# A delta-rule attention block with a hard-swish layer behind it: b of the later units turned by VectorE from quarter transfers, v fetched a block sooner, outputs in one transfer, scan ends copied by ScalarE

## The chip, the cores and the metric

One core of a Trainium2 chip runs the kernel. The metric is the time of one execution on the device, in microseconds. Before the change it is 775.2 us, the median of three runs (773.38 to 775.27).

The engines are named as in the profile: PE is TensorE (PEld its weight loads), DVE VectorE, ACT ScalarE, POOL GpSimd, SP the engine that issues nearly all transfers.

## The reference

```python
# attention: r, k, v, w, a, b are (4 batches, 8 heads, 768 steps, 40); state is (4, 8, 40, 40), from zero
for t in range(S):
    y[:, :, t] = np.einsum('bhd,bhde->bhe', rt, state)
    Sa = np.einsum('bhde,bhe->bhd', state, at)
    state_decay = state * wt[:, :, None, :] - np.einsum('bhd,bhe->bhde', Sa, bt)
    state = state_decay + np.einsum('bhd,bhe->bhde', vt, kt)
# then, on x = y as (3072 tokens, 320):
h = x @ w_in                                   # 320 -> 2048
out = (h * np.clip(h + 3.0, 0.0, 6.0) / 6.0) @ w_out   # 2048 -> 320
```

## The kernel before

**Units.** The 768 steps are cut into blocks of 64 (BL). A unit is one such block of time for a pair of batches: 128 partitions are 2 batches x 64 steps, and the free axis holds 8 heads x 40 features, padded to 64 a head (SLOT). There are NK = 24 units; unit i has time block 2 (i // 4) + (i % 4) // 2 and batch pair i % 2 (`names`). Four units (NU) make a group.

**What is done to a unit.** `prepare(i, F)` needs no state. W turns w (L506) and takes running products along time with a scan on VectorE (L603). gam scans the other way (L614), in place in the edge tile `wm`, then puts together the decays `gam` (G) and their inverses `rgam`: half of each is copied from `wm` (L626 or L628), half from `prods` by GpSimd (L632, L633). A and B turn a and b so that features lie on partitions and time on the free axis, and multiply by G and rg (`at` L650, `bt` L658). F is the product of at and bt (f_by_64, L685); K turns k (L736); factor turns rgam and makes K and B times decay in KBt (L725, GpSimd); E and EV follow. The triangle in F is inverted for a whole group at once by `invert`, some sixty short VectorE steps (L804, L810) that are dealt out between other work ("aside").

`step(i)` carries the state: RT and VT (turns of r and v), R, C, S, U, UT, rS, H, ysn (state and output), then move and move2: eight transfers on SP (L1111 and L1116) that put the unit's output `yg` into `xt` for the feed-forward part. `open` lets the feed-forward stream use it. C ends with a copy of v by GpSimd (L993).

The feed-forward stream takes each unit's xt in two jobs: `expand` (h = xt times win, L1171; the 64 rows left over, "short", L1171 with 64 rows or L1184), hard swish on ScalarE and VectorE (L1193, L1194), and `contract` (L1219), then ob (L1237) and two output transfers on SP (L1243).

**Order.** The order of all engines is fixed when the program is written out: each engine runs its instructions in that order. From unit 8 on (after some 190 us) the work runs in blocks `a_block(m)`, four blocks a unit. In each block, `together` puts the TensorE products of all stages that are due in the order PRODUCTS, then what follows them on the other engines in the order RESULTS; between the blocks, pieces of the feed-forward stream and steps of the inversion are dealt out (`feed`). A unit u begins at block `begins[u]`, 4 blocks apart from unit 12 on, with stages W and gam in the first block, A and B in the second, F and K in the third, E and factor in the fourth, EV in the fifth. Units from 7 on (FAR) have their xt moved in the block of ysn and opened in the next; units 4 to 6 are moved in the block after ysn, which is the block of A and B of a later unit.

"Short" has two forms. `narrow[0](...)` puts it in a block ahead of the stages of HALVES (VT, B, factor): if the block has one of these, as eight pairs of 64x128 matmuls, otherwise as 64x64 quarters (`fours`, L1184).

**Two ways of turning.** Up to unit 7, and for w, k, v later too, TensorE turns a tile through PSUM (`turn_pairs`, `turn_halves`, L516: eight transposes of 64x64 a unit). From unit 8 on, a and r are loaded by quarters (second part of `fetch`, L478): transfers put runs of 80 or 48 features of each head pair to partitions 0 to 31, 32 to 63 and so on, in such places that one VectorE transpose of 32x32 blocks gives the turned tile (`turn_blocks`, L528, L531). b is also read in its plain form, by KBt.

**Transfers.** SP issues them in the order of the program, and each waits for its tile to be free; a waiting one holds all behind it. `fetch("V", i)` of units 9 and later stands at the end of `k_stage`; the slot of `values` that it fills was unit i - 5's, last read by L993.

Of the kernel before, what the change touches and what calls it, by code (L numbers as in the profile page):

```python
# [8 lines left out]
F32 = mybir.dt.float32  # L9
# [22 lines left out]
def kernel(  # L32
# [151 lines left out]
        nc.vector.memset(low[:, i:i + 1], x)  # L184


    AHEAD, FAR = NU + 1, 2 * NU - 1
    PADS = {"W": 1.0, "V4": 1.0}

    def padded(t, name):  # L190
# [18 lines left out]
    nc.vector.memset(start[:], 0.0)  # L209
    nc.vector.memset(start[:].rearrange("p (n i) -> p n i", i=HB + 1)[:, :, 0:1], 1.0)  # L210
    EDGE = 2 * (SCAN + 1)
    area = const.tile([P, EDGE + 3 * H * BL], F32, name="area")
    wms = [area[:, i * (SCAN + 1):(i + 1) * (SCAN + 1)] for i in range(2)]
    for t in wms:
        nc.vector.memset(t, 0.0)
# [235 lines left out]
    def fetch(name, i, engine=None):  # L451

        if i is None or i >= NK:
            return
        x, crossed = {"W": (w, 0), "A": (a, 0), "B": (b, 0), "K": (k, 0), "R": (r, 1),
                      "V": (v, 1)}[name]
        if name == "V":
            t = values[i % AHEAD]
        else:
            t = placed.get((name, i))  # L460
            if (name, i) == ("R", 1):
                t = others["K"]
            if (name, i) == ("W", NU + 1):
                t = values[NU]
            t = t if t is not None else (others if i < 2 * NU and i % 2 and name != "R" else inputs)[name]
        g, p = names[i]
        engines = engine or nc.sync
        if name == "R" and i >= NU or name == "A" and i >= 2 * NU:
            y = x[2 * p:2 * p + 2, :, g * BL:(g + 1) * BL, :]
            n = 2 if name == "R" else 1  # L470
            y = y.rearrange("q (k s j) t e -> s j (q k) (t e)", s=2, j=n).rearrange(
                "s j k (l e) -> s j l k e", e=2 * D)
            for s in range(2):
                for c in range(0, D, L):
                    z = s * SLOT + c
                    to = rooms[name][z:z + L].rearrange("l (j k e) -> l j k e", j=n, e=2 * D)
                    for j in range(n):
                        nc.sync.dma_start(out=to[:, j, :, 0:2 * D - c], in_=y[s, j, :, :, c:])  # L478
            data[i][name + "N"] = t
            return  # L480
        for q in range(2):
            engine = engines[q] if isinstance(engines, tuple) else engines
            y = x[2 * p + q, :, g * BL:(g + 1) * BL, :]
            rows = slice(q * BL, (q + 1) * BL)
            if crossed:
                for s in range(2):
                    engine.dma_start(out=t[rows, 4 * s:4 * s + 4, 0:D],
                                     in_=y[s::2].rearrange("h t e -> t h e"))
            else:
                engine.dma_start(out=t[rows, :, 0:D], in_=y.rearrange("h t e -> t h e"))  # L490
        data[i][name + "N"] = t
# [32 lines left out]
    def turn_blocks(to, name):  # L524

        x = rooms[name].rearrange("p (j k y e) -> p j k y e", j=2, y=2, e=D)[:, :, :, :, 0:L]
        if name == "A":
            nc.vector.transpose(out=to[:].rearrange("p r (q t y) -> p q r y t", q=2, y=2), in_=x)  # L528
            return
        for j in range(2):  # L530
            nc.vector.transpose(out=to[:, 2 * j:2 * j + 2].rearrange("p r (q t y) -> p q r y t", q=2, y=2),  # L531
                                in_=x[:, j].rearrange("p (q r) y t -> p q r y t", q=2))
# [28 lines left out]

    def begun_beside():

        begin = -(-(SCAN + 1) // 16) * 16
        for n, name in enumerate("KB"):
            x = area[:, begin + n * H * JOIN:begin + (n + 1) * H * JOIN]
            nc.gpsimd.memset(x, 0.0)
            beside[name] = x.rearrange("p (h t) -> p h t", h=H)
        beside["E"] = grp.tile([P, H, BL], F32, name="E", tag="U", bufs=1)
        nc.gpsimd.memset(beside["E"][:], 0.0)  # L570
        for name in "rgam", "RT":
            beside[name] = tmp.tile([P, NPR, P], F32, name=name, tag="rgam", bufs=2)

# [7 lines left out]

    def prepare(i, F):
        n, o = i % NU, data[i]
        halves = i >= 2 * NU
        def w_stage():
            wt = turn_pairs(o["WN"])
            yield PE
# [20 lines left out]
        def gam_stage():  # L608

            prods, wm = o["prods"], o["wm"]  # L610
            first = start[:].rearrange("p (n i) -> p n i", i=HB + 1)[:, :, 0]
            nc.vector.reciprocal(first, prods[:].rearrange("p r m i -> p (r m) i")[:, ::-1, HB])
            back = _ap(wm, SCAN, [[-1, SCAN]])
            nc.vector.tensor_tensor_scan(out=back, data0=back, data1=start[:], initial=0.0,  # L614
                                         op0=ALU.mult, op1=ALU.add)
            nc.vector.memset(first, 1.0)
            gam = o["G"] = grp.tile([P, NPR, P], F32, name="gam", tag="gam", bufs=NU + 2)
            rgam = o["rg"] = beside["rgam"] if halves else placed.get(("rgam", i)) or \
                tmp.tile([P, NPR, P], F32, name="rgam", bufs=2)
            gv = gam[:].rearrange("p r (q i) -> p (r q) i", q=2)  # L620
            rv = rgam[:].rearrange("p r (q i) -> p (r q) i", q=2)
            row = 2 * (HB + 1)

            def copy(to, x):
                if i < NU:
                    nc.scalar.activation(out=to, in_=x, func=AF.Copy)  # L626
                else:
                    nc.vector.tensor_scalar(to, x, 1.0, None, ALU.mult)  # L628

            copy(gv[:, :, 0:HB], _ap(o["wm"], HB + 1, [[row, NB], [-1, HB]]))  # L630
            copy(rv[:, :, HB:BL], _ap(o["wm"], HB + 3, [[row, NB], [1, HB]]))
            nc.gpsimd.tensor_copy(gv[:, :, HB:BL], o["prods"][:, :, 1, 0:HB])  # L632
            nc.gpsimd.tensor_copy(rv[:, :, 0:HB], o["prods"][:, :, 0, 0:HB][:, :, ::-1])  # L633
            dec = grp.tile([P, 2, 2, NPR], F32, name="dec", tag="dec", bufs=NU + 2)
            nc.gpsimd.tensor_copy(dec[:].rearrange("p m q r -> p r q m"),
                                  o["prods"][:].rearrange("p (r q) m i -> p r q m i", q=2)[:, :, :, :, HB])
            o["dec"] = dec
            if NU + 1 < i <= 2 * NU:
                fetch("V", i)
            yield from ()  # L640

        def a_stage():
# [4 lines left out]
            if halves:  # L647
                x = at
                turn_blocks(at, "A")
            nc.vector.tensor_tensor(out=at[:], in0=x[:], in1=o["G"][:], op=ALU.mult)  # L650
            fetch("A", following(i))

        def b_stage():
            x = turn_in(o["BN"], halves)
            yield PE
            bt = o["bt"] = turned("bt")
            for y, z, g in zip(parts_of(bt, halves), x, parts_of(o["rg"], halves)):
                nc.vector.tensor_tensor(out=y, in0=z, in1=g, op=ALU.mult)  # L658

# [72 lines left out]
        def k_stage():  # L732
# [1 line left out]
            yield PE  # L734
            kt = o["kt"] = turned("kt")
            nc.vector.tensor_tensor(out=kt[:], in0=x[:], in1=o["rg"][:], op=ALU.mult)  # L736
            if i > 2 * NU:
                fetch("V", i)

        def e_stage():  # L740
            x = scores(o["kt"], o["at"])
# [3 lines left out]
        def ev_stage():  # L745
# [10 lines left out]
            for x in range(2):  # L756
# [1 line left out]
                                     func=AF.Copy)  # L758
            o["EV"] = EV

        return {"W": w_stage, "gam": gam_stage, "A": a_stage, "B": b_stage, "F": f_by_32 if i < 2 * NU else f_by_64,
                "factor": factor_stage, "K": k_stage, "E": e_stage, "EV": ev_stage}

    def in_turn(stages, order):
# [446 lines left out]
    def contract(i, r, gts):  # L1211
# [19 lines left out]
        else:  # L1231
# [5 lines left out]
                nc.scalar.activation(out=ob[:], in_=op[:], func=AF.Copy, scale=1.0 / 6.0)  # L1237
            del ready[i]
            g, p = names[i]
            for q in range(2):  # L1240
                row = (2 * p + q) * T + g * BL
                queue = nc.scalar if q and i == NK - 1 else nc.sync
                queue.dma_start(out=out[row:row + BL, :], in_=ob[half(q)])  # L1243
        yield True


# [201 lines left out]
    for _ in range(18):  # L1448
# [7 lines left out]
    EARLY_STAGES = [["fade"], ["RT", "VT"]]  # L1456
    OWN_STAGES = EARLY_STAGES + [[], ["R", "C", "S"], ["U", "UT", "rS"], ["H"]]
    NEAR_END, FAR_END = [["ysn"], ["move", "move2"]], [["ysn", "move", "move2"], ["open"]]
    AHEAD_STAGES = [["W", "gam"], ["A", "B"], ["F", "K"], ["E", "factor"], ["EV"]]
    CLOSE_STAGES = [["W", "gam"], ["A", "B"], ["F", "K", "factor"], ["E"], ["EV"]]  # L1460


    PRODUCTS = ["W", "S", "K", "VT", "B", "factor",
                "ysn", "EV", "R", "C", "U", "UT", "rS", "H", "E", "F"]
    RESULTS = ["ysn", "W", "VT", "EV", "R", "S", "C", "A", "B", "move", "move2", "open",
               "U", "UT", "rS", "F", "K", "fade", "H", "E", "factor", "RT", "gam"]
    TURNS = PRODUCTS[:3]
    WIDTH = {"R": NPR * D, "U": 512, "UT": 0, "ysn": NPR * JOIN, "EV": NPR * D}
# [40 lines left out]
    def a_block(m):  # L1509

        if coming and begins[coming[0]] == m:
            u = coming.popleft()
            close = coming and begins[coming[0]] < m + BLOCKS
            ahead[u, m] = prepared(u), CLOSE_STAGES if close else AHEAD_STAGES
        i, early = (m + len(EARLY_STAGES)) // BLOCKS + NU, m + len(EARLY_STAGES)
        if m >= 0 and early % BLOCKS == 0 and i < NK:
            own[i, m] = step(i), OWN_STAGES + (NEAR_END if i < FAR else FAR_END)
# [26 lines left out]
    for i in range(NU, NK):  # L1544
        spread[0] = i >= 2 * NU - 1
        for j in range(BLOCKS):
# [18 lines left out]
                rate, inversion = 6.2, 2 + (i < 2 * NU)  # L1565
            feed(rate / 2, inversion)
            m += 1
    for _ in range(2):
        for _ in a_block(m):
            pass  # L1570
        m += 1
# [33 lines left out]
```

## Time and profile before

| | |
|---|---|
| runs | 775.2, 773.38, 775.27 us |
| the profiled execution | 772.7 us |
| its span, first to last instruction | 771.0 us |
| mean granted TensorE clock | 0.956 |
| PE busy | 710.8 us, 92% |
| DVE busy | 508.8 us, 66% |
| ACT busy | 310.4 us, 40% |
| POOL busy | 150.8 us, 20% |
| transfer queue of SP and ACT (q1) | 171552 packets, 45.58 MB, 29.7% of 16 engines' span |
| B's transposes on PE (L516) | 128 |
| copies gam and rgam on DVE (L628) | 20 and 20, medians 0.282 and 0.294 us |

In a row of a timeline stand the start and the length in us, engine, line, operation, tile written <- tiles read, shape and number; in brackets, the engine's idle time before it and what ended it. A row may stand for several instructions of a line that overlap, so that rows of one engine overlap a little; "start to start" is therefore the measure of what a group costs. Rows of SP are the issuing of transfers, not the transfers. "area" is one tile that holds the scan's edges and several work places.

### The profile page before, as it was taken

What the parts mean: (1) busy time and instruction counts of PE and PEld (TensorE: products, weight loads), DVE (VectorE), ACT (ScalarE), POOL (GpSimd) and SP (SyncE); (2) the same over time, 40 slices, a digit from 0 to 9 for tenths busy, and PEclk for the clock granted to TensorE, in tenths of its full rate; (3) what the DMA queues carried; (4) which work ended last, traced back from release to release, by engine and by line L of the source; (5) the groups of instructions that cost most, each with busy time, mean ns of one, the idle gap of its engine ahead of it and who ended that gap; (6) DMA issues with size and microseconds to landing.
All of it is one profiled execution on the core that took longest, in us unless ns stands there. A gap on an engine that the chain in (4) does not pass through costs nothing.

```text
span 771.0 us, 33034 instructions
## 1 busy us (share of the span) xinstructions
PE 710.8 (92%) x14568; PEld 603.1 (78%) x14568; DVE 508.8 (66%) x1027; ACT 310.4 (40%) x644; POOL 150.8 (20%) x303
## 2 busy tenths in 40 slices
PE   4635888999899989999999999999999999999997
PEld 3534777778779778888888888888888888888885
DVE  8899968588557799556798456898436982333210
ACT  2377865232553324552434453234444224322211
POOL 7403210321322211212112121203112010000000
PEclk7956799999999999999999999999999999999999
DMA  9685563420334322233322223313331110110000
GB/s 124 119 179 150 114 170 57 79 43 18 64 65 84 70 55 48 52 71 60 64 52 55 53 62 63 69 37 60 57 72 42 25 24 23 35 35 12 14 16 19
DMA packets 175999, 48.43 MB, mean 63 GB/s; under 512 B 159216, under 2 KB 174576, under 8 KB 175856
## 3 DMA queue, kind: packets, MB, share of 16 engines
q1 hardware_dynamic: 171552, 45.58, 29.7%
q8 instruction: 115, 1.88, 1.0%
q10 hardware_dynamic: 4304, 0.74, 0.7%
q14 instruction: 28, 0.23, 0.1%
HBM read 37.62 MB, written 3.93 MB: 54 GB/s over the span
## 4 chain that ended last, share of the span: by engine, by line
PE 77%; DVE 8%; SPq 5%; issue 3%; DMA 3%; ACT 3%; POOL 0%; DVEq 0%; ACTq 0%; POOLq 0%
PE o L1219 25%; PE h L1171 24%; PE pair L554 4%; PE pair L1064 4%; SPq L490 3%; PE h L1184 2%; PE one L506 2%; PE pair L968 2%; PE pair L927 1%; DVE prod L804 1%; PE pair L1007 1%; PE pair L516 1%; PE pair L752 1%; DVE x L810 1%; PE pair L1023 1%
## 5 line engine op out<-in xcount | busy, mean ns | idle before, releaser
L1171 PE MATMUL h<-xt,win 128*128 128x128 f32 (+1 forms) x2000 | 229.2, 282 | 3.0 <-DVE gt L1194 3.0
L1219 PE MATMUL o<-wout,gt 128*128 128x320 f32 x768 | 230.4, 443 | 0.0
L1171 PEld LDWEIGHTS h<-xt,win 128*128 128x128 f32 (+1 forms) x2000 | 212.9, 193 | 17.5 <-issue 3.1
L1219 PEld LDWEIGHTS o<-wout,gt 128*128 128x128 f32 x768 | 138.6, 190 | 50.3 <-issue 0.2
L1193 ACT ACTIVATE gt<-h,three 128x512 f32<-128x512 f32 x96 | 62.6, 686 | 110.3 <-PE h L1171 88.0
L1194 DVE SCALAR_TENSOR_TENSOR gt<-gt,h 128x512 f32<-128x512 f32 x96 | 61.8, 679 | 62.4 <-ACT gt L1193 62.3
L578 DVE COPY_PREDICATED area<-mask,pair 128x512 f32<-128x512 int32 x56 | 40.5, 726 | 55.2 <-PE pair L554 36.7
L804 DVE TENSOR_TENSOR prod<-x 128x30 f32<-128x30 f32 (+9 forms) x180 | 64.1, 356 | 8.9 <-POOL x L789 3.3
L810 DVE TENSOR_TENSOR x<-x,prod 128x30 f32<-128x30 f32 (+9 forms) x180 | 63.0, 350 | 5.5
L725 POOL TENSOR_TENSOR KBt<-K,rgt 128x320 f32<-128x320 f32 x22 | 19.1, 866 | 142.2 <-ACT rgt L714 134.2
L1071 DVE TENSOR_TENSOR ys<-pair,ys 128x512 f32<-128x512 f32 x20 | 13.8, 690 | 40.5 <-PE pair L1064 40.5
L993 POOL COPY area<-V 128x320 f32<-128x320 f32 x20 | 9.1, 454 | 149.6 <-DVE area L645 53.7
L757 ACT ACTIVATE EV<-pair 64x320 f32<-64x320 f32 x44 | 19.0, 432 | 39.2 <-PE pair L752 38.9
L1064 PE MATMUL pair<-area,KBt 64*64 64x104 f32 x1280 | 32.4, 250 | 0.0
L1237 ACT ACTIVATE ob<-o 128x320 f32<-128x320 f32 x22 | 9.6, 435 | 56.6 <-PE o L1219 35.2
L603 DVE TENSOR_TENSOR_SCAN prods<-area,start 128x528 f32<-128x528 f32 x24 | 29.9, 1250 | 3.4 <-ACT area L599 3.3
L632 POOL COPY gam<-prods 128x256 f32<-128x256 f32 x24 | 12.7, 531 | 99.1 <-DVE prods L603 99.1
L614 DVE TENSOR_TENSOR_SCAN area<-area,start 128x528 f32<-128x528 f32 x24 | 30.6, 1276 | 0.8
L1064 PEld LDWEIGHTS pair<-area,KBt 64*64 64x64 f32 x1280 | 29.9, 133 | 1.5 <-issue 1.4
L872 ACT ACTIVATE tinv<-pair 32x256 f32<-32x256 f32 x48 | 18.0, 375 | 31.9 <-PE pair L862 31.3
L931 DVE TENSOR_TENSOR RR<-pair,EV 128x320 f32<-128x320 f32 x22 | 10.7, 485 | 20.9 <-PE pair L554 13.6
L633 POOL COPY rgam<-prods 128x256 f32<-128x256 f32 x22 | 23.9, 1084 | 0.0
(289 smaller groups left out, 1078.5 us busy)
## 6 DMA issues: line engine op xcount, KB each, us to landing
V<-in_v_dram SPq DMA_DIRECT2D x96, 40.0 KB
out_dram<-ob SPq DMA_DIRECT2D x47, 80.0 KB
R<-in_r_dram SPq DMA_DIRECT2D x92, 40.0 KB
B<-in_b_dram SPq DMA_DIRECT2D x42, 80.0 KB
K<-in_k_dram SPq DMA_DIRECT2D x42, 80.0 KB
W<-in_w_dram SPq DMA_DIRECT2D x37, 80.0 KB
A<-in_a_dram SPq DMA_DIRECT2D x37, 80.0 KB
xt<-yg SPq DMA_DIRECT2D x72, 40.0 KB
```

The costliest lines, as they stand in the source:

```text
L554: nc.tensor.matmul(out=o[i][half(q), n ^ (2 * q * placed), :], lhsT=lhs[half(i, D), n ^ (2 * q * swap), half(q)], rhs=rhs[half(i, D), n, h ...
L578: nc.vector.copy_predicated(out=x[:].rearrange("p (i h) t -> p i h t", i=2), mask=mask8, data=o[2])
L603: nc.vector.tensor_tensor_scan(out=prods[:].rearrange("p r m i -> p (r m i)"), data0=wm[:, 0:SCAN], data1=start[:], initial=0.0, op0=ALU.m ...
L614: nc.vector.tensor_tensor_scan(out=back, data0=back, data1=start[:], initial=0.0, op0=ALU.mult, op1=ALU.add)
L633: nc.gpsimd.tensor_copy(rv[:, :, 0:HB], o["prods"][:, :, 0, 0:HB][:, :, ::-1])
L804: nc.vector.tensor_tensor(out=pv, in0=_ap(x[:], (i + 1) * L + i, [[L, n], [0, i]]), in1=_ap(x[:], i * L, [[0, n], [1, i]]), op=ALU.mult,)
L810: nc.vector.tensor_tensor(out=rest, in0=rest, in1=pv, op=ALU.add)
L1064: nc.tensor.matmul(out=both[q][half(s), pr, :], lhsT=o[name][half(q), h * D:h * D + SLOT], rhs=beside[name][half(q), 4 * rs + 2 * (s ^ (q ...
L1171: nc.tensor.matmul(out=hp[c][:, i, :], lhsT=lhsT, rhs=rhs, start=(begun[c] == 0), stop=(begun[c] == 3 * NQ - 1))
L1193: nc.scalar.activation(out=gt[:], in_=hp[c][:], func=AF.Relu, bias=three[:], scale=1.0)
L1194: nc.vector.scalar_tensor_tensor(out=gt[:], in0=gt[:], scalar=6.0, in1=hp[c][:], op0=ALU.min, op1=ALU.mult)
L1219: nc.tensor.matmul(out=op[:], lhsT=gts[c][:, n, :], rhs=wout[:, c * HJ + r * NQ + n, :], start=((split or r == 0) and c == 0 and n == 0), ...
```

## The change

- b of units 12 to 23 (QUARTERS = 12) is loaded a second time, by quarters like a, into a new part of `area` (`rooms["Bq"]`, 640 columns at TAIL, cleared once by GpSimd in `begun_beside`), and turned by VectorE (`turn_blocks(bt, "Bq")`), which then multiplies from SBUF. Stage B of these units is called Bq; it isn't among PRODUCTS, and HALVES doesn't name it. The plain transfer of b stays, for KBt. Each unit's quarters (four transfers) are fetched at the end of stage Bq of the unit before, those of unit 12 ahead of block 12.
- `fetch("V", i)` of units 9 on stands in `a_stage`, ahead of `fetch("A", ...)`, and not in `k_stage`.
- An output is one transfer of 128 rows in place of two of 64, but for the last unit.
- The two copies from the scan's edges into gam and rgam, for units 8 on, are a stage "edge" of their own, done by ScalarE, first in RESULTS, in the block of A and B; before, VectorE did them in stage gam.

```diff
-    AHEAD, FAR = NU + 1, 2 * NU - 1
+    AHEAD, FAR, QUARTERS = NU + 1, 2 * NU - 1, 3 * NU
...
-    area = const.tile([P, EDGE + 3 * H * BL], F32, name="area")
+    PLACE = -(-(SCAN + 1) // 16) * 16
+    TAIL = PLACE + 2 * H * (BL + D)
+    area = const.tile([P, TAIL + 2 * H * D], F32, name="area")
...
-                      "V": (v, 1)}[name]
+                      "V": (v, 1), "Bq": (b, 0)}[name]
...
-            t = placed.get((name, i))
+            t = rooms.get(name) if name[1:] else placed.get((name, i))
...
-        if name == "R" and i >= NU or name == "A" and i >= 2 * NU:
+        if name == "R" and i >= NU or name == "A" and i >= 2 * NU or name[1:]:
...
-        if name == "A":
+        if name != "R":
             nc.vector.transpose(out=to[:].rearrange("p r (q t y) -> p q r y t", q=2, y=2), in_=x)
...
+        rooms["Bq"] = area[:, TAIL:]
+        nc.gpsimd.memset(rooms["Bq"], 0.0)
...
-        halves = i >= 2 * NU
+        halves, by_quarters = i >= 2 * NU, i >= QUARTERS
...
-            def copy(to, x):
-                if i < NU:
-                    nc.scalar.activation(out=to, in_=x, func=AF.Copy)
-                else:
-                    nc.vector.tensor_scalar(to, x, 1.0, None, ALU.mult)
-
-            copy(gv[:, :, 0:HB], _ap(o["wm"], HB + 1, [[row, NB], [-1, HB]]))
-            copy(rv[:, :, HB:BL], _ap(o["wm"], HB + 3, [[row, NB], [1, HB]]))
+            o["edges"] = [(gv[:, :, 0:HB], _ap(o["wm"], HB + 1, [[row, NB], [-1, HB]])),
+                          (rv[:, :, HB:BL], _ap(o["wm"], HB + 3, [[row, NB], [1, HB]]))]
+            if not halves:
+                yield from edge_stage()
...
+        def edge_stage():
+
+            for to, x in o["edges"]:
+                if i < NU or halves:
+                    nc.scalar.activation(out=to, in_=x, func=AF.Copy)
+                else:
+                    nc.vector.tensor_scalar(to, x, 1.0, None, ALU.mult)
+            yield from ()
+
...
             nc.vector.tensor_tensor(out=at[:], in0=x[:], in1=o["G"][:], op=ALU.mult)
+            if i > 2 * NU:
+                fetch("V", i)
             fetch("A", following(i))

         def b_stage():
-            x = turn_in(o["BN"], halves)
+            x = [None] if by_quarters else turn_in(o["BN"], halves)
             yield PE
             bt = o["bt"] = turned("bt")
+            if by_quarters:
+                x = parts_of(bt, halves)
+                turn_blocks(bt, "Bq")
+                fetch("Bq", following(i))
...
             nc.vector.tensor_tensor(out=kt[:], in0=x[:], in1=o["rg"][:], op=ALU.mult)
-            if i > 2 * NU:
-                fetch("V", i)
...
-            for q in range(2):
-                row = (2 * p + q) * T + g * BL
-                queue = nc.scalar if q and i == NK - 1 else nc.sync
-                queue.dma_start(out=out[row:row + BL, :], in_=ob[half(q)])
+            rows = out.rearrange("(b t) m -> b t m", t=T)[2 * p:2 * p + 2, g * BL:(g + 1) * BL, :]
+            if i < NK - 1:
+                nc.sync.dma_start(out=rows, in_=ob[:])
+            else:
+                for q in range(2):
+                    (nc.scalar if q else nc.sync).dma_start(out=rows[q], in_=ob[half(q)])
...
-    AHEAD_STAGES = [["W", "gam"], ["A", "B"], ["F", "K"], ["E", "factor"], ["EV"]]
-    CLOSE_STAGES = [["W", "gam"], ["A", "B"], ["F", "K", "factor"], ["E"], ["EV"]]
+    AHEAD_STAGES = [["W", "gam"], ["edge", "A", "B"], ["F", "K"], ["E", "factor"], ["EV"]]
+    CLOSE_STAGES = [["W", "gam"], ["edge", "A", "B"], ["F", "K", "factor"], ["E"], ["EV"]]
...
-    RESULTS = ["ysn", "W", "VT", "EV", "R", "S", "C", "A", "B", "move", "move2", "open",
+    RESULTS = ["edge", "ysn", "W", "VT", "EV", "R", "S", "C", "A", "B", "Bq", "move", "move2", "open",
...
-            ahead[u, m] = prepared(u), CLOSE_STAGES if close else AHEAD_STAGES
+            order = CLOSE_STAGES if close else AHEAD_STAGES
+            ahead[u, m] = prepared(u), [[x + "q" if x == "B" and u >= QUARTERS else x for x in y] for y in order]
...
             m += 1
+            if m == BLOCKS * (QUARTERS - AHEAD - NU):
+                fetch("Bq", QUARTERS)
```

## The prediction

> **What bounds the kernel now.** I read the chain of work that ended last, then the busy time by stretches of 30 us, then the timelines of single blocks.
>
> ```profile
> PE 77%; DVE 8%; SPq 5%; issue 3%; DMA 3%; ACT 3%; POOL 0%; DVEq 0%; ACTq 0%; POOLq 0%
> ```
> The chain is TensorE's for 77%. By stretches (columns: PE, PEld, DVE, ACT, POOL busy, granted clock, DMA share, GB/s):
>
> ```profile
> 180.00:210.00 30.00, 27.68 (x557) 23.03 (x557) 21.12 (x45) 13.07 (x29) 9.57 (x16) 1.00 0.21 41
> 210.00:240.00 30.00, 30.00 (x737) 24.25 (x730) 20.29 (x40) 12.93 (x32) 5.73 (x13) 1.00 0.39 75
> 270.00:300.00 30.00, 27.07 (x448) 22.88 (x448) 28.08 (x74) 8.76 (x19) 3.87 (x8) 0.94 0.21 42
> 300.00:330.00 30.00, 30.00 (x756) 26.13 (x755) 19.77 (x33) 15.31 (x34) 7.07 (x11) 1.00 0.35 67
> 480.00:510.00 30.00, 30.00 (x478) 25.41 (x477) 26.74 (x61) 8.13 (x17) 6.57 (x15) 1.00 0.33 67
> ```
> From 210 us to its last matmul TensorE has no idle time, but for 2.9 us between 270 and 300, where VectorE (28.1 of 30) inverts the triangles of a group. All the change touches lies after 190 us. So work taken from TensorE counts in full, work moved among VectorE, ScalarE and GpSimd counts only where TensorE waits for it, and a transfer counts only if TensorE comes to wait for it.
>
> **B's turns leave TensorE.** One unit's turn, in the PE timeline:
>
> ```profile
> 335.06 1.16 PE L1171 MATMUL h<-xt,win 64*128 64x128 f32 x16
> 336.06 0.41 PE L516 MATMUL pair<-ident,B 64*128 64x64 f32 x8
> 336.39 0.68 PE L927 MATMUL pair<-state,at 40*64 40x40 f32 x32
> 414.37 1.10 PE L1184 MATMUL h<-xt,win 64*64 64x128 f32 x32
> 415.29 1.60 PE L1064 MATMUL pair<-area,KBt 64*64 64x104 f32 x64
> ```
> From start to start, the sixteen narrow h matmuls and the eight transposes take 1.33 us (335.06 to 336.39). With B gone these blocks have no member of HALVES, and L1184's 32 quarter matmuls take the place of the sixteen; they take 0.92 us (414.37 to 415.29), so 0.41 is saved. That holds for six of units 12 to 23 (12, 14 and so on). In the other six, B follows the state's transposes and takes 0.39 us start to start. 6 x 0.41 + 6 x 0.39 = 4.8 us. Unit 12's 0.41 falls at 274 us, just before a wait for VectorE, so it only lengthens that wait: **-4.4 us** is left.
>
> **VectorE and ScalarE.** Units 12 to 23 each gain a 128x512 transpose on VectorE, at 0.69 (L528's row); bt's product stays at 0.69 (L650, from SBUF) against 0.68 (L658). Units 8 to 23 lose two copies at 0.28 and 0.29 (L628), which come back on ScalarE at 0.41 (L626, units 0 to 3): 13 us more on an engine that is 40% busy. What waits: VectorE's clearing of the scan's edges (L645) now waits for ScalarE's copies, and behind it stand at, bt and the inversion's steps; on ScalarE the copies stand ahead of S (L954). In unit 13 the scan ends at 309.9, ScalarE's gt at 311.3, so the copies end near 312.2; L645 ran at 313.1, so nothing waits. S moves from 311.2 to 312.1, and its reader (L1023) runs at 317.1. bt is ready 0.7 later, at 315.8, and F (L685) reads it at 317.6, or 0.4 earlier now: 1.4 us to spare. Unit 16, amid an inversion, has 1.4 likewise (397.3 against 398.7). I take 0; if the cover is gone, each us past it costs a us per unit.
>
> In one place VectorE does end TensorE's wait, in unit 12's blocks:
>
> ```profile
> 270.45 0.28 DVE L628 TENSOR_SCALAR gam<-area 128x256 f32<-128x256 f32 x1
> 270.66 0.29 DVE L628 TENSOR_SCALAR rgam<-area 128x256 f32<-128x256 f32 x1
> 270.87 1.27 DVE L1194 SCALAR_TENSOR_TENSOR gt<-gt,h 128x512 f32<-128x512 f32 x2
> ...
> 280.46 1.07 PE L752 MATMUL pair<-V,E 64*64 64x40 f32 x32 [1.91 <-DVE area L645]
> ```
> VectorE works without a pause from 264 to 280 us. Without the copies gt starts at 270.41, so all that follows, TensorE's restart too, comes **0.46 us** sooner. GpSimd's new clearing of 128x640 costs 0.6 us by the neighbours (128x832 in 0.76, 128x512 in 0.53). It falls at 194 us ahead of "scale", which VectorE awaits; two copies less (0.55) follow in that chain, so TensorE's wait at 199.8 grows by 0.1. Bounds 0 and 0.6; I take 0.1.
>
> **The queues.** Each transfer on SP takes time to issue: A's quarters 1.80 for four when nothing holds them, V's four 2.7 to 3.7, an output 0.6. The unit from 325.6 to 350.6 us has 21.7 us of issuing; four quarters more and one output less make it 23. It still fits, as the pause before B and K (2 to 10 us, waiting for GpSimd's KBt) takes it up. The issues saved on outputs thus bring 0, and V a block sooner brings 0, since no wait names a V transfer after 210 us. But both new groups stand ahead of one move of xt:
>
> ```profile
> 272.00 1.22 SPq L1243 DMA_DIRECT2D out_dram<-ob  x2
> 281.05 1.80 SPq L478 DMA_DIRECT2D A<-in_a_dram  x4
> 282.89 3.09 SPq L1111 DMA_DIRECT2D xt<-yg  x4
> 286.02 2.48 SPq L1116 DMA_DIRECT2D xt<-yg  x4
> 288.61 3.18 SPq L487 DMA_DIRECT2D V<-in_v_dram  x4
> ```
> These are unit 6's moves. For units from 7 on (FAR) xt is moved a block earlier, ahead of A's block; for unit 6 it follows unit 12's a_stage, and the changed order is V (waiting for GpSimd's read of that slot, L993, which ended at 280.92), A, B's quarters, xt. Start 280.92 - 0.46 = 280.5; V 2.75, A 1.80, quarters 1.80 (A's row; at most 3.15, A's longest), xt 3.09, with 0.05 between groups: the fourth issue ends at 290.1. In the trace of before it ended at 285.98 and landed at 287.14 by the landing events, 1.16 later. So xt lands at 291.2. TensorE read it first at 290.61; it would now be there at 290.15. It waits 1.1 us, and goes on **0.6 us** later than before, the 0.46 counted. Bounds: V at 3.7 and the quarters at 3.15 give 2.9; the quickest issues (V 2.65) 0.5. Unit 4's xt also gets V ahead of it (2.8 us, less some 0.8 for outputs merged), but had 5.3 us between landing and first read (L1111's last issue ended at 224.6, first h at 231.06), so 3.3 are left; unit 5 has V ahead of it already. Cost 0.
>
> Sum: -4.4 + 0.6 + 0.1 = **-3.7 us**. The profiled execution took 772.7 us (span 771.0 and 1.7 around it), which gives 769.0. That execution was quicker than the runs shown (773.38 to 775.27), so against their median of 775.2 I predict **771.5**, 0.5% less.
>
> **The clock, and a rule against this change.** After the 1.91 us wait at 280.46 eight h matmuls took 2.07 us, where 1.16 is usual; the stretch 280 to 284 has a granted clock of 0.57, so 4 x 0.43 = 1.7 us were lost. Waits of 1.21 (199.84) and 1.11 (205.60) lost none. The Trainium skill (TensorE: Matmul & The Clock Gate, "Part 1: The HAM clock gate") says that the array's clock is halved after an idle window of about 3.4 us, free-running, and given back after a busy one; by that, whether a wait costs more depends on where it falls in the window. The trace agrees on the halving, but a wait of 1.9 us sufficed; by the rule the sum is -3.7 or, with a slow window, -2.0. The new wait for xt is 1.1 us, but 2.8 if the earlier one is spared its slow window (290.15 - 1.7 = 288.45, xt still at 291.2).
>
> **Rivals.**
> 1. The slow window follows xt's wait: +1.7, so -2.0, or 773.2: within 0.3%. For it: the kernel pays such a window already after 1.91 us. Against: not after 1.2.
> 2. xt does not hold TensorE, the row of V or of the landing being shorter than taken: -4.4 - 0.46 + 0.1 = -4.8, or 770.4. Against: even the quickest rows leave a wait.
> 3. Slower: F waits for bt in every unit. Place: L685 in units 12 to 23; it decides once VectorE's at and bt come over 1.4 us later than worked out, for instance if ScalarE, standing at gt or ob, reaches the copies that late. With 1 us past that point, 12 - 3.7 = +8.3, or 783.5. For it: a new wait VectorE on ScalarE, and VectorE is 90% busy in inversions. Against: in units 12, 13, 14 and 16 ScalarE had ended what stands ahead of the copies when VectorE came.
> 4. It doesn't do what it says: TensorE's place is taken by short waits for VectorE or ScalarE of 0.3 us a unit, as VectorE has only 1.5 us to catch up after each inversion (417 and 528 us, where it waits for TensorE): -0.5, or 774.7.
>
> **Chances.** Forecast 0.50, rival 1 0.23, rival 2 0.10, rival 3 0.11, rival 4 0.06. A measurement of this kernel can tell about 0.3% (2.3 us) from no change: faster = 0.50 + 0.10 = 0.60, within = 0.23 + 0.06 = 0.29, slower 0.11. The range leaves out rival 3; at the bottom it goes from the quickest run shown less rival 2 (773.38 - 4.8 = 768.6), at the top to rival 4 (774.7) and xt's upper bound: 768.6 to 775.2.
>
> **What will show it.** Right: 32 transposes of B at L516 instead of 128; 32 more copies gam and rgam on ScalarE; twelve transposes bt at 0.69; on SP around 281 V, A, area, xt; TensorE idle about 1.1 us before h near 291, ended by xt's DMA; none after 300 us. Wrong: idle time at F ended by VectorE (rival 3), a clock under 1.00 after 291 (rival 1), no wait at 291 (rival 2), or TensorE's busy time no less than 4 us lower while the span stays (rival 4).

## The result, and the profile after

The changed kernel takes 770.3 us (median of 13 runs) against 774.7 us of the kernel before (13 runs beside it): a ratio of 0.994, 95% interval 0.9924 to 0.9953. The profiled execution took 768.3 us (span 766.6, granted clock 0.967), against 772.7 (771.0, 0.956). The forecast was 769.0 for the profiled execution and 771.5 for the median. The number came out; several of its steps did not, and in unit 12's blocks their errors cancelled, which is luck.

The page's chain of waits, and the busy time by stretches (PE, PEld, DVE, ACT, POOL, clock, DMA share, GB/s) of the changed kernel:

```profile
PE 77%; DVE 9%; SPq 5%; DMA 4%; issue 2%; ACT 1%; POOL 1%; DVEq 0%; POOLq 0%; ACTq 0%
```
```profile
270.00:300.00 30.00, 26.28 (x454) 22.25 (x453) 28.04 (x73) 9.30 (x21) 2.54 (x7) 0.94 0.31 63
300.00:330.00 30.00, 29.74 (x747) 25.85 (x746) 18.71 (x29) 15.77 (x36) 6.44 (x11) 1.00 0.38 74
```
TensorE still sets the end. The stretch 270 to 300 has more idle time than before (3.7 against 2.9 us) and the same clock of 0.94, so the gain does not come from there. It comes later; after 345 us no idle time of TensorE over 0.15 us is left in either profile. The block that the prediction showed at 335.06 and 336.06, in the PE timeline after:

```profile
335.36 1.10 PE L1196 MATMUL h<-xt,win 64*64 64x128 f32 x32
336.28 0.62 PE L939 MATMUL pair<-state,at 40*64 40x40 f32 x32
```
The 32 quarter matmuls take 0.92 us, start to start, in place of 1.33 with the narrow ones and B's transposes: the 0.41 forecast.

To see where time is won I compared the starts of o's 768 matmuls, one by one, with those in the first profile of before, and took the change of the distance over four stretches (us, minus is quicker; the bounds are times of before, each taken at the first of these matmuls behind it). Each row is one profile; the kernels are those of the experiments below:

| kernel | 0–253 | 253–297 | 297–345 | 345–766 |
|---|---|---|---|---|
| changed | -0.7 | +0.8 | +0.5 | -4.2 |
| changed, once more | -0.1 | +0.8 | -0.5 | -4.3 |
| before, once more | +0.3 | -1.6 | +1.4 | +0.5 |
| no quarters | +0.4 | -2.0 | +4.8 | -0.2 |
| quarters alone | +2.0 | +1.4 | 0.0 | -3.5 |
| edge copies on VectorE | -0.6 | +1.7 | -0.3 | -3.2 |
| xt first | -0.4 | -3.2 | +3.4 | -3.7 |
| PSUM turn kept | +0.7 | -0.6 | +0.1 | -3.8 |
| v late | -1.6 | +0.4 | -0.1 | -2.7 |
| two outputs | -0.3 | 0.0 | -0.2 | -3.8 |
| clearing late | +0.9 | +0.6 | +0.2 | -4.0 |
| three edits | +3.5 | -0.6 | +2.2 | -3.7 |
| xt first in the kernel before | +2.2 | 0.0 | +2.3 | +0.1 |

After 345 us, where the turns of units 15 to 23 lie, the change is worth 4.2 us; ahead of that it moves waits about. In unit 12's blocks (253 to 297) the waits are others than in before. The PE timeline and SP's issues of the changed kernel:

```profile
276.01 0.68 PE L764 MATMUL pair<-V,E 64*64 64x40 f32 x32
...
282.18 0.98 PE L699 MATMUL pair<-bt,at 40*64 40x64 f32 x32 [0.26 <-DVE bt L672]
283.09 2.42 PE L1231 MATMUL o<-wout,gt 128*128 128x320 f32 x8
288.94 6.52 PE L1183 MATMUL h<-xt,win 128*128 128x128 f32 x48 [3.44 <-DVE prod L816]
```
```profile
276.70 2.61 SPq L489 DMA_DIRECT2D V<-in_v_dram  x4
279.94 2.47 SPq L480 DMA_DIRECT2D A<-in_a_dram  x4
282.50 1.88 SPq L480 DMA_DIRECT2D area<-in_b_dram  x4
284.42 3.11 SPq L1123 DMA_DIRECT2D xt<-yg  x4
```
EV (L764, the product of V and E), which waited 1.91 us for VectorE, waits for nothing and runs 4.45 us sooner. C ahead of it (L556, RT and VT), which waited 0.68, waits for nothing either. F (L699) now waits 0.26 us for bt, as in rival 3, in this one unit. TensorE is ready for h at 285.5 and stands 3.44 us. The label names VectorE's inversion, but xt's fourth move was issued by 287.53, and h starts 1.41 later; the experiment with xt first shows that xt was it. The 48 matmuls then take 6.52 us where 4.83 is usual. The granted clock is 0.50 from 288.9 to 292.3; such a stretch is called a half-clock window below, and this one costs 1.7.

### The profile page after: what moved, and what is told of

It is laid out like the page before. It is cut to its first block, busy times and chain, and to the rows that moved or that the text cites. A ratio compares the mean times of both kernels' runs of the same rounds, so it can differ in the third digit from the quotient of the medians.

```text
span 766.6 us, 33042 instructions
## 1 busy us (share of the span) xinstructions
PE 705.6 (92%) x14568; PEld 598.0 (78%) x14568; DVE 509.1 (66%) x1007; ACT 320.2 (42%) x676; POOL 141.7 (18%) x304
## 3 DMA queue, kind: packets, MB, share of 16 engines
q8 instruction: 115, 1.88, 1.0%
## 4 chain that ended last, share of the span: by engine, by line
PE 77%; DVE 9%; SPq 5%; DMA 4%; issue 2%; ACT 1%; POOL 1%; DVEq 0%; POOLq 0%; ACTq 0%
PE o L1231 26%; PE h L1183 24%; PE pair L556 4%; PE pair L1076 4%; PE h L1196 3%; SPq L492 3%; PE one L508 2%; DVE x L822 2%; DVE prod L816 2%; PE pair L939 1%; PE pair L980 1%; PE pair L1019 1%; PE pair L1035 1%; PE one L961 1%; PE pair L874 1%
## 5 line engine op out<-in xcount | busy, mean ns | idle before, releaser
L1183 PE MATMUL h<-xt,win 128*128 128x128 f32 (+1 forms) x1904 | 221.4, 282 | 6.1 <-DVE prod L816 3.4
L1183 PEld LDWEIGHTS h<-xt,win 128*128 128x128 f32 (+1 forms) x1904 | 206.5, 193 | 19.2 <-DVE prod L816 3.9
L739 POOL TENSOR_TENSOR KBt<-K,rgt 128x320 f32<-128x320 f32 x22 | 19.1, 866 | 200.7 <-ACT rgt L728 165.5
L1196 PE MATMUL h<-xt,win 64*64 64x128 f32 x800 | 27.6, 275 | 0.0
```

What stands on the lines that cost most here:

```text
L1183: nc.tensor.matmul(out=hp[c][:, i, :], lhsT=lhsT, rhs=rhs, start=(begun[c] == 0), stop=(begun[c] == 3 * NQ - 1))
L1196: nc.tensor.matmul(out=hp[c][half(z), i, :], lhsT=y[:, half(z)], rhs=xt[half(c), 2, :], start=(begun[c] == 0), stop=(begun[c] == 3 * NQ - 1))
```

## The experiments

Theory 1: B's transposes off TensorE are the gain, and unit 12's blocks trade EV's wait for one for xt. Theory 2: the gain comes from the other edits.

**No quarters.** The other three edits stay.

```diff
-    AHEAD, FAR, QUARTERS = NU + 1, 2 * NU - 1, 3 * NU
+    AHEAD, FAR, QUARTERS = NU + 1, 2 * NU - 1, 6 * NU
```


> The changed kernel with b of all units turned by TensorE again; V a block sooner, merged outputs and edge copies on ScalarE stay. Theory 1 (the gain is B's transposes off TensorE, eleven units after 300 us at about 0.36): the gain is gone, ratio to the kernel before 0.999 to 1.001; in the profile the wait of 3.44 us ahead of h at 289 is gone and EV waits about 1.9 us for VectorE again, as it shares its PSUM turn with B's again. Theory 2 (the gain comes from the other three edits: fewer issues on SP, fewer VectorE copies, v sooner): ratio 0.994 to 0.996.

Measured: 0.999 (0.9965 to 1.0016). The gain after 345 us is gone (-0.2), and EV's wait is back:

```profile
280.50 0.68 PE L764 MATMUL pair<-V,E 64*64 64x40 f32 x32 [1.92 <-DVE area L653]
```
Theory 1 holds here. Of the +4.8 between 297 and 345, 1.60 us are a stall in F, of which more at the end, 1.7 a half-clock window after it, and 0.81 a wait for VectorE at L851, which the second profile of before has too.

**Quarters alone.** The changed kernel with the three edits of the next two experiments together: edge copies on VectorE, v fetched in k_stage, two outputs a unit.

> The kernel before with b by quarters alone: V in its old block, two output transfers a unit, edge copies on VectorE. Theory 1: ratio to before 0.994 to 0.996, as the whole change, with TensorE waiting some 3 to 3.5 us for xt near 289 (A's fetch ahead of xt waits for VectorE's transpose at 279.9, so V ahead of A costs nothing; the copies back on VectorE make it about 0.5 later). Theory 2: 0.998 to 1.000.

Measured: 0.9989 (0.9967 to 1.0012). Theory 1's number failed. After 345 us the gain is there (-3.5), but at 200 us TensorE waits longer, and a half-clock window follows:

```profile
200.16 0.75 PE L873 MATMUL pair<-zs,tt 32*32 32x32 f32 x64 [1.51 <-DVE area L652]
200.85 3.46 PE L1182 MATMUL h<-xt,win 128*128 128x128 f32 x16
```
That wait is 1.09 in the changed kernel, and the sixteen h matmuls take 2.05 there. The window is chance in part: a wait of 1.50 or 1.51 at this place has none behind it in three other profiles. The wait for xt is 3.96, not 3.44. By the ratios the quarters need one of the other edits: neither part alone gives a difference that can be told from none.

**Edge copies on VectorE again.** All else as changed; "edge" also leaves the two lists of stages.

```diff
-            if not halves:
-                yield from edge_stage()
+            yield from edge_stage()
...
-                if i < NU or halves:
+                if i < NU:
```


> The changed kernel with the copies of the scan ends of units 8 to 23 on VectorE again. Theory 1: within 1 us of the changed kernel, ratio to before 0.993 to 0.996; at unit 12 VectorE's chain, and with it A's fetch and xt, 0.4 later; from 300 us on nothing waits for VectorE. Rival (VectorE's time matters now that it has B's transposes): two copies of 0.28 in twelve units, up to 6.7 us more, ratio up to 1.002.

Measured: 0.9976 (0.9959 to 0.9992), 0.0037 above the changed kernel's ratio; with the two intervals taken as independent that is 0.0015 to 0.0059, or 1.2 to 4.6 us. Theory 1 missed it. The trace has 2.0 us in three places: 0.41 at 199 (1.50 against 1.09), 0.64 at xt (4.08 against 3.44; VectorE's chain, hence A's fetch and xt behind it, is later: A is issued at 280.44, xt at 285.44), and 1.0 after 345 us. But 0.8 comes back between 297 and 345, and the last o is only 1.2 us later than in the changed kernel's first profile; the second has 3.77 at xt, so part of the 0.64 is chance too. The 1.0 comes in four steps of 0.16 to 0.36. The largest is F of unit 15, in the changed kernel and with the copies on VectorE:

```profile
365.26 0.65 PE L1035 MATMUL pair<-RT,S 40*64 40x64 f32 x32
365.72 0.65 PE L699 MATMUL pair<-bt,at 40*64 40x64 f32 x32
```
```profile
365.51 0.65 PE L1034 MATMUL pair<-RT,S 40*64 40x64 f32 x32
366.28 0.69 PE L698 MATMUL pair<-bt,at 40*64 40x64 f32 x32
```
F starts 0.77 after the product ahead of it, not 0.46, and 0.05 after VectorE has ended bt; in the changed kernel bt is ready 0.51 ahead of F. In the blocks of units 16 and 20 the copies cost 0.2 each, and there moving them saves the same 0.2 without quarters.

**V late, two outputs.** Two kernels, each with one part undone. In the first these lines go from a_stage back to the end of k_stage; in the second the last lines replace the branch:

```diff
-            if i > 2 * NU:
-                fetch("V", i)
...
-            if i < NK - 1:
-                nc.sync.dma_start(out=rows, in_=ob[:])
+            for q in range(2):
+                (nc.scalar if q and i == NK - 1 else nc.sync).dma_start(out=rows[q], in_=ob[half(q)])
```

> The changed kernel with v fetched in its old block. Theory 1: no change, ratio to before 0.993 to 0.995; at unit 12 A's fetch starts at 279.9 when VectorE's transpose ends, V or not, so xt's wait stays 3.4 us. Rival (V ahead of A delays xt): xt 2.6 us sooner, no slow window, ratio 0.988 to 0.990.

> The changed kernel with two output transfers a unit again. Theory 1: no change, ratio to before 0.993 to 0.995, as SP's issues are hidden. Rival (SP's time matters): slower than the changed kernel by 2 us or more, ratio over 0.996, with TensorE waiting for a transfer after 300 us.

Measured: 0.9951 (0.9927 to 0.9975) and 0.9936 (0.9912 to 0.9959). Both are about as expected: neither part can be told from nothing in the time. But v late leaves a wait that the changed kernel hasn't:

```profile
568.63 3.01 SPq L489 DMA_DIRECT2D V<-in_v_dram  x4
```
```profile
574.46 0.66 PE L764 MATMUL pair<-V,E 64*64 64x40 f32 x26 [1.22 <-DMA V<-in_v_dram]
```
The quarters (3.80 us of issuing there) push the end of V's last issue to 571.64. But that transfer lands only at 574.41, 2.8 us later; the three before it took 1.7, which would have meant 573.3, and TensorE was ready at 573.24. Quarters alone, with v in the old block too, has no wait there. So the wait is mostly one late landing, and that the quarters need V a block sooner is not shown.

**PSUM turn kept.** B's stage takes its columns of PSUM as before, but writes nothing to them. Three more lines, not shown, put the stage back among PRODUCTS under the name B and keep "short" in its quarter form.

```diff
+            if by_quarters:
+                ps_pair(NPR, BL)
```


> The changed kernel, but B's stage of units 12 to 23 still takes its turn of PSUM columns without writing or reading them, so that the later products of a block get the banks that they had before. Theory 1 (EV waits no more because it got another bank once B took no columns): EV near 280 waits 1 to 2 us for VectorE again, TensorE reaches h about 2.5 us later and its wait for xt shrinks from 3.44 to under 1; the time stays within 1 us of the changed kernel, ratio to before 0.993 to 0.996, since xt sets the end of these blocks either way. Rival (EV is free because VectorE, without the two copies, comes sooner): EV waits for nothing and the wait for xt stays 3.4.

Measured: 0.9915 (0.9883 to 0.9947). The waits in its PE timeline:

```profile
276.15 0.69 PE L556 MATMUL pair<-RT,VT 40*64 40x64 f32 x32 [1.13 <-DVE E L581]
...
280.11 0.68 PE L766 MATMUL pair<-V,E 64*64 64x40 f32 x32 [1.28 <-DVE RR L945]
...
290.64 4.90 PE L1185 MATMUL h<-xt,win 128*128 128x128 f32 x48 [1.80 <-DVE x L824]
```
VectorE's work is that of the changed kernel, and yet C and EV wait again: the bank decides, not VectorE's speed. The kernel shows why. `ps_pair` hands out parts of a tile of 2 x 512 columns, of which there are two by turns. B's 256 and R's 160 leave no room for C's 256; without B, R and C fit together, and EV gets the other tile. It is not quite the wait of before: there EV began (280.46) when VectorE had read C (L578 ends at 280.41), here when it had read R (L945 ends at 280.05). The long wait is now three of 1.1 to 1.8 us, at 1.00 of the clock, and these blocks are 1.4 us quicker than in the changed kernel, where the window alone costs 1.7. xt's wait shrank to 1.80, not under 1. The ratio lies below the expected range, which its interval still reaches.

**xt first.** One word order; in the program it moves unit 6's eight moves ahead of V, A and the quarters, and nothing else.

```diff
-"S", "C", "A", "B", "Bq", "move", "move2", "open",
+"S", "C", "move", "move2", "A", "B", "Bq", "open",
```


> The changed kernel with the eight moves of xt issued ahead of V, A and B's quarters in the one block where they followed them (unit 6). Theory 1 (TensorE's 3.44 us at 289 are a wait for xt, which stands behind A and the quarters on SP, and the half-clock window after it loses 1.7 more): 5.1 us less than the changed kernel, ratio to before 0.987 to 0.989, no idle time and full clock at 285 to 292. Theory 2 (that wait is for VectorE's inversion steps L816, as the profile labels it): no change, ratio 0.994, the wait still there.

Measured: 0.9919 (0.9888 to 0.995). The 3.44 us and the half-clock window are gone, which settles that TensorE waited for xt. But little of the 5.1 us stays won: the ratio is 0.002 below the changed kernel's, within both intervals. PE, then VectorE:

```profile
286.89 4.93 PE L1183 MATMUL h<-xt,win 128*128 128x128 f32 x48 [0.68 <-DVE gt L1206]
...
299.56 1.16 PE L1183 MATMUL h<-xt,win 128*128 128x128 f32 x8 [1.66 <-DVE gt L1206]
...
306.85 0.74 PE L851 MATMUL pair<-tb,F 32*32 32x32 f32 x64 [0.80 <-DVE state L1085]
```
```profile
294.37 0.86 DVE L816 TENSOR_TENSOR prod<-x 128x150 f32<-128x150 f32 x1
295.27 0.86 DVE L822 TENSOR_TENSOR x<-x,prod 128x150 f32<-128x150 f32 x1
...
298.83 1.28 DVE L1206 SCALAR_TENSOR_TENSOR gt<-gt,h 128x512 f32<-128x512 f32 x2
```
ScalarE had ended its gt at 293.1; VectorE comes to its own part at 298.83, behind the inversion's steps. Of the 1.66 us that TensorE waits there, 1.1 come from the two steps shown, which take 0.86 where 0.32 is usual: GpSimd multiplies into KBt (L739) at the time, which in the changed kernel falls behind the inversion (297.65). VectorE, busy 28.0 of 30 us, is the next bound: 4.0 us are won up to 297, and 2.9 given back by 345.

**xt first in the kernel before.** The same reorder there.

> The kernel before with the moves of xt ahead of A's fetch in unit 6's block. Theory 1: no change, ratio 0.999 to 1.001: there TensorE did not wait for xt but for VectorE at EV. Rival (xt held TensorE before too): 0.995 or less.

Measured: 1.0002 (0.9985 to 1.002). Before, xt held nothing; the change made it late by sending TensorE there sooner.

**The same kernels once more.**

> The changed kernel once more, unaltered, to tell chance from cause. Theory 1: from 253 us on the trace repeats (idle time of 3.2 to 3.6 us ahead of h near 289, none over 0.5 after it, and 4.0 to 4.3 us less than before between 345 us and the end), while the place of TensorE at 253 us differs from the first profile's by up to 1.5 either way, since the waits and half-clock windows of the loading phase fall by chance. Rival (the 0.7 us that the changed kernel was ahead at 253 us belong to the change): ahead by 0.5 to 0.9 again. Ratio to before 0.993 to 0.995.

> The kernel before once more. Theory 1: EV's wait of 1.9 us near 280 is there again, with a half-clock window after it or without; TensorE's place at 253 us differs by up to 2 from the first profile's. Rival: it repeats within 0.3.

Measured: the changed kernel 0.9941 (0.9909 to 0.9973), with the wait for xt at 3.77 (a little above the expected 3.6), a half-clock window after it, no wait over 0.5 later, and -4.3 after 345. Its place at 253 us is -0.1 instead of -0.7, so that lead was chance. Before once more: EV's wait of 1.91 again, this time without a half-clock window, hence its -1.6; and +1.4 and +0.5 in the later stretches (0.81 and 0.45 us of them waits at L839). One profile of a kernel is thus good to about 1.6 us a stretch.

**Clearing late**, and **three edits**. In the first the clearing moves from begun_beside to the first fetch that needs it; the second has that, xt first, and quarters from unit 13 on (the last two lines).

```diff
-        nc.gpsimd.memset(rooms["Bq"], 0.0)
...
+                nc.gpsimd.memset(rooms["Bq"], 0.0)
                 fetch("Bq", QUARTERS)
...
-    AHEAD, FAR, QUARTERS = NU + 1, 2 * NU - 1, 3 * NU
+    AHEAD, FAR, QUARTERS = NU + 1, 2 * NU - 1, 3 * NU + 1
```


> The changed kernel with GpSimd's clearing of 128x640 put off from 193 us to the fetch that needs it, near 271 us. Theory 1 (it delays scale, and so VectorE's state and TensorE): of TensorE's three waits between 194 and 205 (0.68, 1.09 and 1.10) some 0.6 to 0.9 in all goes, and nothing near 271 waits for it; ratio to before 0.991 to 0.994. Rival (other work ends those waits): they stay, ratio 0.993 to 0.995.

> The changed kernel with xt's moves first in unit 6's block, the clearing put off to 271 us, and unit 12's b turned by TensorE (quarters from unit 13 on), which takes a transpose of 0.7 us from VectorE in the midst of an inversion. Theory 1 (with xt early the stretch from 280 to 310 is bound by VectorE's inversion, so TensorE's 0.41 more is free there and VectorE's 0.7 less counts): ratio to before 0.988 to 0.991. Rival (unit 12's turn back on TensorE brings EV's wait of 1.9 us back, with a half-clock window): 0.992 to 0.995.

Measured: 0.9917 (0.9891 to 0.9942) and 0.9911 (0.9885 to 0.9936). With the clearing late, the wait of 0.68 at 194 is gone and those of 1.09 and 1.10 stay; nothing waits for it at 266. The wait of 0.68 is also missing with v late and with the PSUM turn kept, where the clearing is early but TensorE reaches that place 0.6 us later after VectorE's transposes. What the clearing does is plainer at GpSimd's `scale`: it ends 3.22 us after those transposes with the clearing early, 2.66 with it late. With three edits EV waits 1.91 us again and xt for nothing, as the rival had it, though no half-clock window follows; its +3.5 ahead of 253 us holds a wait of 1.52 for b's transfer, with a half-clock window behind it. The medians beside each other on one chip were 769.7 (changed kernel), 769.3 and 769.7: none of the variants is shown to be quicker than the changed kernel.

## Why the prediction came out, step by step

- **B's turns, -4.4.** Right in mechanism and place, and nearly in size. The turns of units 15 to 23 lie after 345 us (those of 13 and 14 ahead of it); at the prediction's prices these nine are 5 x 0.39 + 4 x 0.41 = 3.6. Measured are 4.2 and 4.3, in steps of 0.39 to 0.66, against 0.2 without quarters. Quarters with the copies on VectorE give 3.2, and quarters alone 3.5. So 0.7 to 1.0 of the 4.2 belong to the edge copies.
- **Edge copies, "I take 0" but for 0.46 at unit 12.** Wrong: with the quarters they are worth 1.2 to 4.6 us by the ratios, 1.2 by the last o of the two first profiles. The spare time of 1.4 us at units 13 and 16 was nearly right (1.20 and 1.17), but behind unit 12's blocks the tightest units are 15 and 19, with 0.51. I looked at two units and not for the tightest, and never asked what would be left with the copies on VectorE: 0.05 and 0.09. Rival 3, F waiting for bt, is there in small when they stay. That the copies also bring the wait at 199 us down from 1.50 to 1.09, below every wait that had a half-clock window behind it, may explain why the ratios show more than one trace; this is not shown.
- **"TensorE's restart 0.46 sooner", read of xt at 290.15.** This step failed. EV's wait did not move, it vanished, as B took no columns and EV got a bank that had long been free. TensorE was ready at 285.5. I had listed what B's turn costs TensorE and not what it holds in PSUM.
- **xt's landing at 291.2.** By the landing events it came at 288.70, 1.17 after the end of the fourth issue, where 1.16 was taken. V was issued in a gap of SP from 276.70, as GpSimd's copy ran at 269.99 (L1005) and not at 280.47 (L993); A's start at 279.94 follows the end of VectorE's transpose. In before the copy began when VectorE had written C into `area`, where the copy writes too. In all eleven profiles of kernels made from the changed one it is over 8 us ahead of that write, without quarters and with quarters alone too; what they share, and no run undid, is the wider `area`. That the width is the cause was not tried. The issue times taken for xt (3.09) and the quarters (1.80) held at 3.11 and 1.88.
- **Net of these blocks, +0.6.** Measured +0.8 twice, partly by chance: both wrong steps shift the same wait, and before's profile holds a half-clock window there as well. Against before's second profile, without one, these blocks cost 2.4, of which 0.9 and 1.9 come back by 345 us in the two profiles of the changed kernel. That the sum of the two wrong steps lands near +0.6 is luck.
- **Half-clock window after xt's wait, rival 1 at 0.23.** It came, in both profiles of the changed kernel. The condition that the text gave for a wait of 2.8 was the one that mattered; the wait was 3.4.
- **GpSimd's clearing, 0.1.** Right. From the end of VectorE's transposes of the inversion to the matmuls at L874 (L862 before), where the wait of 1.21 was, it is 8.22 us in before, 8.37 in the changed kernel, 7.81 with the clearing late and 8.79 with the copies on VectorE. So the clearing costs 0.56, the copies' move gives 0.42 back, and 0.14 is left. The new wait of 0.68 lies ahead of that place and shortens the wait there.
- **Outputs and v, 0 each.** Right in time.
- The last o's result is 3.9 us sooner, the span 4.4: the last output landed 0.5 quicker, which the change does not touch.

## What to carry to other kernels

Work that leaves an engine also leaves its buffers: look which later product inherits the bank and whose wait ends with it. When a wait goes, find out from the queue what lands next and from the other engines who is next; here xt stood 3.4 us behind, and the inversion on VectorE right behind xt. Before calling work free, look for the unit with the least spare time, not for a typical one: here 0.51 us, which the copies would have used up.

## What the runs showed of the hardware

In the 14 profiles, after 115 us, none of TensorE's 80 waits of 0.6 to 1.45 us was followed by a half-clock window. Of 25 waits of 1.46 to 1.92 us eight were, and of seven of 2.95 to 4.08 all seven. Each window is recorded as 3.413 us, and costs about 1.7 us of matmul time. The Trainium skill (TensorE: Matmul & The Clock Gate, "Part 1: The HAM clock gate") gives a free-running window of 3413 ns; the length agrees, and that of EV's five waits of 1.91 or 1.92 us two were followed by a half-clock window and three not fits a window that does not start with the wait. That an idle window is needed does not agree: a wait of 1.48 us sufficed.

A step of the inversion on VectorE that begins while GpSimd multiplies into KBt (0.86 us a product) ends only 0.05 to 0.2 us after that product: 0.86 us in place of 0.32 with xt first, 0.83 in place of 0.25 at 160 us in the changed kernel. The like stands in every profile.

F of unit 13 stalls after eight or nine of its 32 matmuls, with nothing named that it waits for ("issue"): 0.26 us in one of the changed kernel's two profiles, 1.60 without quarters, 0.77 with xt first, 1.59 with xt first in the kernel before; with three edits 1.09, after seventeen; and not at all in the other nine. It does not go with the change. The place is the same in all five: number 11714 of TensorE's recorded instructions, weight loads counted too, from 0. In all 14 profiles TensorE has 53 idle stretches over 0.2 us after 40 us that are labelled "issue", and each begins where that number, divided by 256, leaves 193 or 194. So they hang on a place in the instruction stream that comes every 256 instructions, and on chance, as few of these places have one. What happens there, the trace does not say.
